# Attention and Snake feed-forward on one core: h tiles multiplied in pairs ahead of their Sin, matmuls grouped by tile shape, loads a chunk ahead, first chunks squared on ScalarE

## The chip, the cores and the metric

The kernel runs on one core of a Trainium2 chip. The time is that of the device, in microseconds (us); most executions of one kernel agree within one to two per cent. Each kernel was run several times, and one of the runs left a profile. The core has a matmul engine (TensorE, "PE" in the profile, with "PEld" for its weight loads), VectorE (DVE), ScalarE (ACT), GpSimd (POOL) and SyncE, which here only issues DMAs (SPq). Matmul results go to PSUM, here a ring of four pairs of banks.

## The reference

Eight batches, twelve heads, 448 tokens, head size 64. First attention with normalized q and k, then a feed-forward on the 3584 tokens, with the "snake" function between two matrix products.

```python
def rmsnorm(x, g):
    return x / np.sqrt(np.mean(x * x, axis=-1, keepdims=True) + 1e-06) * g
q_n, k_n = rmsnorm(q, g_q), rmsnorm(k, g_k)
scores = 1.0 / np.sqrt(64) * np.matmul(q_n, k_n.transpose(0, 1, 3, 2))
attn = np.exp(scores - max)            # row by row
attn = attn / (sum(attn) + 1e-09)
x = np.matmul(attn, v)                 # then to (3584 tokens, 768)

h = x @ w_in                           # 768 x 2048: the first product
s = np.sin(alpha * h)
g = h + s * s / (alpha + 1e-09)
out = g @ w_out                        # 2048 x 768: the second product
```

All inputs and the output are float32; the kernel multiplies in bf16.

## The kernel before

Per batch there is an *attention stretch* of six head pairs and then a *first product* with its snake. The second product of a batch is cut into steps of two matmuls ("fillers") that are put between the attention matmuls of the next batch. The normalization of the next batch's q and k ("norm tasks", three chunks of four heads per batch) runs in the background of the attention stretch. These are the parts that the change and the argument touch; cuts are marked with "...".

```python
    def norm_tasks(ci):                      # one chunk: 4 heads of q and of k
        def square(w):    ... nc.gpsimd.tensor_mul(st[w], qk[ci][:, w], qk[ci][:, w])
        def fold_g():         nc.gpsimd.tensor_mul(qk[ci][:, 1], qk[ci][:, 1], gg.to_broadcast([P, 2 * NJ, D]))
        def reduce(w):        nc.vector.reduce_sum(st["ms"][:, w, :], st[w], axis=AX.X)
        def rsqrt():      ... # Ln and Exp on ScalarE
        def scale(w):     ... nc.vector.tensor_mul(st["n"][...], qk[ci][:, w, js], st["inv"][...].to_broadcast(...))   # twice
        def transpose():  ... nc.sync.dma_start_transpose(out=qkT[pi]..., in_=st["n"]...)                             # twice
        return [lambda: square(0), lambda: square(1), lambda: (reduce(0), fold_g()), lambda: reduce(1), rsqrt,
                lambda: scale(0), lambda: scale(1), transpose]
...
    def attend(pi):
        av = bank_pair("av")
        for bank in range(2):                # bank 0: exp x v, bank 1: exp x ones (the row sums)
            for t in range(NT + 1):
                for hi in range(2):
                    ...                      # t < NT: tiles of 128 x 64, t == NT: tiles of 64 x 64
                    nc.tensor.matmul(av[r, bank, :S], lhsT, rhs, start=(t == 0), stop=(t == NT))
...
    def first_product(b):
        EARLY = 4                            # these are multiplied before the last head pair's xT is there, all but their last k tile
        ...
        for m in range(MT):                  # 16 h tiles of 128 x 448; two share a PSUM bank pair
            if m < EARLY:
                mm(tiles[m // 2], m, [KT - 1])
            else:
                if m % 2 == 0:
                    tiles[m // 2] = bank_pair("hps")
                mm(tiles[m // 2], m, range(KT))                        # 6 matmuls
            late.append(snake(b, tiles[m // 2][:, m % 2, :S], m))      # Sin on ScalarE, square, then VectorE
            if len(late) > 1:
                late.popleft()()
...
        for p in range(NP):                  # six head pairs
            scores(pi, 0); fill(part[1]); scores(pi, 1); bg(per_slot); fill(part[2] - part[1])
            if p:
                attend(pi - 1)
            fill(part[3] - part[2]); bg(per_slot); scores(pi, 2)
            fill(part[4] - part[3]); bg(per_slot); scores(pi, 3)
            fill(part[5] - part[4]); bg(per_slot)
            ...                              # batch 0: loads of w_in in four steps, then v and w_out
        bg(len(background)); fill(len(fillers))
        attend(b * NP + NP - 1)
        first_product(b)
```

## Time and profile before

The kernel took 692.86 us in the median of three runs. From the start times of the matmuls the span of the profiled run divides as follows (a stretch ends where the first matmul of the next one starts):

| stretch | before | after |
|---|---|---|
| until the first scores | 39.5 | 34.6 |
| attention of batch 0 | 72.4 | 44.2 |
| eight first products | 240.4 | 146.0 |
| attention of batches 1 to 6 | 275.6 | 256.7 |
| attention of batch 7 (nothing left to normalize) | 38.3 | 35.7 |
| last second product and store | 26.4 | 26.4 |
| span | 692.6 | 543.7 |

The page of the profile, its head. The digits are tenths of busy time in 40 slices of the span; PEclk is the clock granted to TensorE, and a half-clock window is a stretch in which the clock record grants half of full speed. In the profile's lines the tiles have the program's names: qkn and qkT are the normalized q and k before and after the transpose, sc the scores, expT their exponentials, av the product with v, xT the attention's result, hps the PSUM tiles of the first product, s and g_sb those of the snake, ops the accumulator of the second product.

```profile
span 692.6 us, 7553 instructions
...
PE 518.8 (75%) x2816; PEld 209.2 (30%) x2816; DVE 249.8 (36%) x352; ACT 342.1 (49%) x544; POOL 266.7 (39%) x253
...
PE   0043436789978995888878987888878986899786
...
PEclk9999656998999998999999995998999997999899
```

A PE that is 75% busy looks nearly full, but the figure is an average over stretches with different limits, and a matmul counts as busy longer than it keeps its successor waiting (352 ns of modelled duration against 189 ns from start to start).

The timeline of one period of a first product: start, duration, engine, line, operation, what it writes and reads, number of instructions, and in brackets the idle time before it and its releaser.

```profile
198.15 2.43 PE L261 MATMUL hps<-xT,w_in_sb 128*128 128x448 bf16 x12 [0.78 <-ACT s L242]
...
199.54 0.63 ACT L242 ACTIVATE s<-hps,alpha_sb 128x448 f32<-128x448 f32 x1 [1.44 <-PE hps L261]
...
200.69 0.62 ACT L242 ACTIVATE s<-hps,alpha_sb 128x448 f32<-128x448 f32 x1
201.35 2.43 PE L261 MATMUL hps<-xT,w_in_sb 128*128 128x448 bf16 x12 [0.78 <-ACT s L242]
```

The period is 201.35 - 198.15 = 3.20 us for 12 matmuls that need 12 x 0.189 = 2.27. PE multiplies the odd half of a pair and the even half of the next one, and then cannot start that pair's odd half until the Sin at 200.69 has read the even half: the two engines take turns. The waits view (engine and line, what it waited for, total us, times, longest) sums it up.

```profile
PE hps L261 <- ACT s L242: 56.1, 64, 1.7
...
PE sc L206 <- DMA qkT<-qkn: 51.7, 3, 39.5
...
PE hps L261 <- DVE xT L236: 10.5, 3, 3.9
```

In the attention the tightest stretch is batch 7. One head pair there, PE's timeline; the column after the names is the part of the array that a matmul uses, rows x columns, so "128*64" is half an array and two such matmuls run side by side (in this trace they start 4 ns apart).

```profile
611.54 1.06 PE L230 MATMUL av<-expT,vb 128*64 128x448 bf16 x8
612.54 1.06 PE L230 MATMUL av<-expT,ones 128*64 128x448 bf16 x8
613.54 0.50 PE L298 MATMUL ops<-w_out_sb,g_sb 128*128 128x384 bf16 x2
613.97 0.36 PE L206 MATMUL sc<-qkT 64*128 64x448 bf16 x2
614.26 0.82 PE L298 MATMUL ops<-w_out_sb,g_sb 128*128 128x384 bf16 x4
615.02 0.38 PE L208 MATMUL sc<-qkT 64*64 64x448 bf16 x2
615.33 0.82 PE L298 MATMUL ops<-w_out_sb,g_sb 128*128 128x384 bf16 x4
```

No line has an idle time in brackets, so PE bounds this stretch; from attend to attend it takes 6.31 us. Yet two second-product matmuls take 613.97 - 613.54 = 0.43 us before the shape changes, where 2 x 0.163 = 0.33 would do, and a pair of scores takes 0.29 us instead of 0.19. Each change of the tile shape costs about 0.1 us, and a head pair has 13 of them (an attend alone starts four of them: its 64x64 part comes once per bank).

### The profile page before, as it was taken

Reading aid. Unit: us, or ns where it says so; the run is one execution under the profiler, and the core shown is the slowest. Engines: PE = TensorE matmul, PEld = TensorE weight load, DVE = VectorE, ACT = ScalarE, POOL = GpSimd, SP = SyncE. Lnnn points to the kernel's source line nnn. Section 1 sums busy time; section 2 is a strip of 40 time slices with the busy share of each in tenths; the row PEclk is TensorE's granted clock in tenths of the full one; section 3 lists DMA queues with packets and bytes.
Section 4 is the critical chain, followed back from the end, with each engine's and each line's share of the span. In section 5 each row is a group of like instructions: output and inputs, shape, how many; then the busy total and the mean of one; then the engine's idle time right before and its main releaser. Section 6 shows DMA issues by size and latency. Waiting matters only on the chain.

```text
span 692.6 us, 7553 instructions
## 1 busy us (share of the span) xinstructions
PE 518.8 (75%) x2816; PEld 209.2 (30%) x2816; DVE 249.8 (36%) x352; ACT 342.1 (49%) x544; POOL 266.7 (39%) x253
## 2 busy tenths in 40 slices
PE   0043436789978995888878987888878986899786
PEld 0011102333333332333333332332333332333244
DVE  0543233344443425333543433333533333221331
ACT  0042226565656555565556644664556544765530
POOL 4842447283328303453436332543437332100210
PEclk9999656998999998999999995998999997999899
DMA  9259769865526544165407344355407342001002
GB/s 190 18 69 150 126 125 142 162 40 126 116 66 41 126 104 102 13 74 136 126 2 77 89 109 96 24 68 140 117 1 73 94 111 43 1 24 45 1 23 70
DMA packets 114406, 56.41 MB, mean 81 GB/s; under 512 B 93377, under 2 KB 110785, under 8 KB 114369
## 3 DMA queue, kind: packets, MB, share of 16 engines
q1 hardware_dynamic: 64432, 44.13, 27.6%
q0 software_dynamic: 49936, 11.80, 18.8%
q8 instruction: 22, 0.36, 0.2%
q14 instruction: 16, 0.12, 0.1%
HBM read 45.69 MB, written 11.01 MB: 82 GB/s over the span
## 4 chain that ended last, share of the span: by engine, by line
PE 45%; ACT 16%; POOL 14%; DMA 9%; DVE 7%; issue 5%; SPq 3%; DVEq 0%; ACTq 0%; POOLq 0%
PE hps L261 16%; PE ops L298 16%; ACT s L242 10%; PE av L230 9%; POOL sq L159 6%; DMA qk<-in_q_dram 6%; POOL vb L105 4%; ACT s L247 4%; PE sc L206 3%; POOL vb L109 3%; DVE qkn L177 3%; SPq L185 3%; DMA vb<-in_v_dram 2%; DVE ms L165 2%; PE sc L208 1%
## 5 line engine op out<-in xcount | busy, mean ns | idle before, releaser
L261 PE MATMUL hps<-xT,w_in_sb 128*128 128x448 bf16 x768 | 174.5, 378 | 66.6 <-ACT s L242 56.1
L298 PE MATMUL ops<-w_out_sb,g_sb 128*128 128x384 bf16 x896 | 186.7, 336 | 1.6 <-ACT expT L210 1.6
L159 POOL TENSOR_TENSOR sq<-qk 128x896 f32<-128x896 f32 x48 | 81.5, 1733 | 185.7 <-DMA qk<-in_q_dram 176.3
L210 ACT ACTIVATE expT<-sc 128x896 bf16<-128x896 f32 x144 | 126.6, 916 | 38.5 <-PE sc L206 37.5
L245 POOL TENSOR_TENSOR s<-s 128x448 f32<-128x448 f32 x64 | 59.7, 932 | 197.5 <-ACT s L242 182.1
L250 DVE SCALAR_TENSOR_TENSOR g_sb<-s,inv_alpha_sb,hps 128x448 bf16<-128x448 f32 x128 | 81.4, 677 | 140.8 <-ACT s L242 135.9
L242 ACT ACTIVATE s<-hps,alpha_sb 128x448 f32<-128x448 f32 x128 | 80.4, 628 | 103.3 <-PE hps L261 103.3
L261 PEld LDWEIGHTS <-w_in_sb 128*128 128x128 bf16 x768 | 78.1, 103 | 161.2 <-issue 105.9
L206 PE MATMUL sc<-qkT 64*128 64x448 bf16 x288 | 55.2, 385 | 66.0 <-DMA qkT<-qkn 51.7
L298 PEld LDWEIGHTS <-g_sb 128*128 128x128 bf16 x896 | 72.4, 99 | 77.4 <-issue 46.6
L165 DVE TENSOR_REDUCE ms<-sq 128x14 f32<-128x896 f32 x48 | 51.6, 1082 | 116.7 <-POOL sq L159 116.6
L236 DVE TENSOR_TENSOR xT<-av,rec 128x448 bf16<-128x448 f32 x48 | 29.8, 621 | 130.9 <-ACT rec L233 130.9
L177 DVE TENSOR_TENSOR qkn<-qk,inv 128x448 bf16<-128x448 f32 x96 | 64.3, 727 | 6.1 <-ACT inv L170 5.8
L230 PE MATMUL av<-expT,vb 128*64 128x448 bf16 (+1 forms) x384 | 57.7, 399 | 5.8 <-ACT expT L212 4.7
L232 ACT ACTIVATE rec<-av 128x448 f32<-128x448 f32 x48 | 26.1, 543 | 72.6 <-PE av L230 72.4
L169 ACT ACTIVATE inv<-ms,eps 128x28 f32<-128x28 f32 x24 | 7.6, 318 | 104.1 <-DVE ms L165 104.1
L230 PE MATMUL av<-expT,ones 128*64 128x448 bf16 (+1 forms) x384 | 56.9, 398 | 0.0
L162 POOL TENSOR_TENSOR qk<-qk,gg 128x896 f32<-128x896 f32 x24 | 50.4, 2100 | 1.9
L206 PEld LDWEIGHTS <-qkT 64*128 64x128 bf16 x288 | 15.0, 94 | 112.4 <-issue 59.6
L208 PE MATMUL sc<-qkT 64*64 64x448 bf16 x96 | 19.3, 395 | 28.5 <-ACT expT L210 22.1
L247 ACT ACTIVATE s<-s 128x448 f32<-128x448 f32 x64 | 36.9, 576 | 2.0
L105 POOL DMA_DIRECT2D vb<-in_v_dram x48 | 36.4, 788 | 0.8 <-POOLq L378 0.8
(21 smaller groups left out, 191.2 us busy)
## 6 DMA issues: line engine op xcount, KB each, us to landing
qk<-in_q_dram SPq DMA_DIRECT2D x24, 448.0 KB, 4.3
qk<-in_k_dram SPq DMA_DIRECT2D x24, 448.0 KB, 4.5
out_dram<-osb SPq DMA_DIRECT2D x56, 192.0 KB, 2.7
vb<-in_v_dram POOLq DMA_DIRECT2D x48, 96.0 KB, 3.8
w_in_sb<-in_moe_w_in_dram POOLq DMA_DIRECT2D x16, 192.0 KB, 5.5
w_out_sb<-in_moe_w_out_dram POOLq DMA_DIRECT2D x1, 3072.0 KB, 19.6
vb<-in_v_dram POOLq DMA_DIRECT2D x48, 16.0 KB, 2.7
qkT<-qkn SPq DMA_TRANSPOSE x48, 3.9
```

Of the source, the lines that this page charges most:

```text
L105: nc.gpsimd.dma_start(out=vb[b][jj * 64:jj * 64 + 64, t * H:(t + 1) * H, :], in_=tok[2 * t + jj])
L159: nc.gpsimd.tensor_mul(st[w], qk[ci][:, w], qk[ci][:, w])
L165: nc.vector.reduce_sum(st["ms"][:, w, :], st[w], axis=AX.X)
L177: nc.vector.tensor_mul(st["n"][:, w, :, hi, :], qk[ci][:, w, js], st["inv"][:, w, js].unsqueeze(2).to_broadcast([P, NJ, D]))
L206: nc.tensor.matmul(sc[:, hi, :S], kt[r, t * P:(t + 1) * P], qt[r, :], start=True, stop=True)
L210: nc.scalar.activation(expT[pi][:, 2 * t:2 * t + 2, :], sc[:, :, :S], ACT.Exp, scale=SCALE)
L230: nc.tensor.matmul(av[r, bank, :S], lhsT, rhs, start=(t == 0), stop=(t == NT))
L242: nc.scalar.activation(s1, hps, ACT.Sin, scale=alpha_sb[:, m, :])
L247: nc.scalar.activation(s2, s1, ACT.Square)
L250: nc.vector.scalar_tensor_tensor(g_sb[:, m, (b % 2) * S:(b % 2 + 1) * S], s2, inv_alpha_sb[:, m, :], hps, op0=ALU.mult, op1=ALU.add)
L261: nc.tensor.matmul(ps[:, m % 2, :S], w_in_sb[:, kt, m * P:(m + 1) * P], x[:, kt, :], start=(kt == 0), stop=(kt == KT - 1))
L298: nc.tensor.matmul(st["ps"][:, half, :HALF], lhsT, w_out_sb[:, m, half * HALF:(half + 1) * HALF], start=(m == 0), stop=(m == MT - 1))
```

## The change

The intent: let PE run through the first product without waiting for Sin; put matmuls of one tile shape together; start the work on q and k earlier; load with fewer, larger DMAs.

```diff
-    def load_qk(ci):
+    def load_qk(ci, eng=nc.sync):          # a chunk now takes its heads hi-major, v and w_in alike: longer runs per DMA
 ...
-    load_qk(1)
-    load_qk(2)
+    load_qk(1, nc.scalar)
+    load_qk(2, nc.scalar)
 ... # load_v: 4 DMAs per batch instead of 12; load_w_in: 2 DMAs in all instead of 16
-    def norm_tasks(ci):
+    def norm_tasks(ci, first=False):
 ...
-            nc.gpsimd.tensor_mul(st[w], qk[ci][:, w], qk[ci][:, w])
+            if first:
+                nc.scalar.activation(st[w], qk[ci][:, w], ACT.Square)
+            else:
+                nc.gpsimd.tensor_mul(st[w], qk[ci][:, w], qk[ci][:, w])
 ... # fold_g of the first chunks on VectorE; scale(1) in three instructions, for the new order of k's tokens
-        return [lambda: square(0), lambda: square(1), lambda: (reduce(0), fold_g()), lambda: reduce(1), rsqrt,
-                lambda: scale(0), lambda: scale(1), transpose]
+        if first:
+            return [lambda: square(1), lambda: (square(0), fold_g()), lambda: (reduce(1), reduce(0)), rsqrt,
+                    lambda: scale(0), lambda: scale(1), transpose]
+        return [lambda: (square(0), square(1)), fold_g, lambda: None, lambda: reduce(0), lambda: reduce(1), lambda: None,
+                rsqrt, lambda: (scale(0), scale(1), transpose())]
 ...
-        for bank in range(2):
-            for t in range(NT + 1):
+        for t in range(NT + 1):
+            for bank in range(2):
 ...
-        EARLY = 4
+        EARLY = 2
 ...
-        for m in range(MT):
-            if m < EARLY:
-                mm(tiles[m // 2], m, [KT - 1])
-            else:
-                if m % 2 == 0:
-                    tiles[m // 2] = bank_pair("hps")
-                mm(tiles[m // 2], m, range(KT))
-            late.append(snake(b, tiles[m // 2][:, m % 2, :S], m))
+        for i in range(MT // 2):
+            if i >= EARLY:
+                tiles[i] = bank_pair("hps")
+            for m in (2 * i, 2 * i + 1):
+                mm(tiles[i], m, [KT - 1] if i < EARLY else range(KT))
+            for m in (2 * i, 2 * i + 1):
+                late.append(snake(b, tiles[i][:, m % 2, :S], m))
 ...
+    gate = const.tile([P, 1], F32)
+    nc.gpsimd.tensor_copy(gate, qk[0][:, 0, 0, 0:1])      # GpSimd's loads wait for the first q
     load_v(0)
-    background.extend(norm_tasks(0))
-    bg(len(background))
     load_alpha()
-    for ci in range(1, NC):
-        background.extend(norm_tasks(ci))
+    load_w_in()
+    for ci in range(2):
+        for task in norm_tasks(ci, first=True):
+            task()
+    background.extend(norm_tasks(2, first=True))
 ...
-                background.append(lambda ci=ci: load_qk(ci))
-                background.extend(norm_tasks(ci))
+                tasks = norm_tasks(ci)
+                if ci + 1 < NC * B:
+                    tasks[0] = lambda t=tasks[0], ci=ci: (t(), load_qk(ci + 1))
+                background.extend(tasks)
 ...
-            scores(pi, 0); fill; scores(pi, 1); bg; fill; attend(pi - 1); fill; bg; scores(pi, 2); fill; bg; scores(pi, 3); fill; bg
+            scores(pi, 0); scores(pi, 1); attend(pi - 1); scores(pi, 3); bg; fill; bg; scores(pi, 2); fill; bg; fill; bg
```

(The last two lines stand for the loop body, one call per line in the kernel.)

## The prediction

> **What bounds the kernel now.** The program alternates eight attention stretches (each carrying the second product of the batch before) with eight first products. From the start times of the matmuls: first scores at 39.5 us; batch 0's attention to 111.9; attention of batches 1 to 7 together 314 us (44.0, 46.8, 44.7, 46.8, 46.6, 46.7, 38.3); the first products together 240 us (26.7 to 36.3); a last second product and store, 26 us.
>
> - *First product.* Timeline: 12 matmuls per h tile pair every 3.21 us, though matmuls follow each other at 0.189 us, so 12 need 2.27. The waits view: hps matmuls wait for the Sin 64 times, 56.1 us. A pair's odd half is written only after the even half's Sin has read the tile. ScalarE's own work is 1.8 us per pair.
> - *Attention.* Batch 7 shows the PE bound: 6.31 us per head pair without idle in the timeline. Of it 12 tiled pairs x 0.187 + 16 second-product matmuls x 0.163 = 4.84; the rest is 13 changes of tile shape, each about 0.1 us longer than a step without one (0.26 to 0.31 against 0.16 to 0.19). The Trainium skill (TensorEngine Tiling (Array Packing), Key Properties) says that a mode change drains the engine; the trace agrees. Batches 1 to 6 add 4 to 6 us: v loads hold POOL 8 us, then the squares, so reduce, rsqrt and the Exps behind it come late.
> - *Start.* POOL issues v loads until 20.3, then squares; scores start at 39.5. Batch 0 is a chain of qk loads, transposes, squares, reductions (PE busy 30.9 of 72.4 us, clock 0.77).
>
> **What the change does.**
> 1. First product: PE-bound at 2.27 us per pair, 96 matmuls = 18.1; I expect 18.7 per batch, 150 in all: -90 us, all on the chain.
> 2. Shape changes per head pair from 13 to 6: 4.84 + 6 x 0.105 = 5.5 us (6.4 with 128 fillers). v loads: 4 issues instead of 12; norm work spaced, loads a chunk ahead. With 3 us at each start for the last Sins and the table load: 38, 43 and 35.5 us per batch, 278 together: -35.
> 3. Start: qk0 lands at 8 to 9 us, Square on ACT, gg at 10 to 12 (was 11.7), then DVE fold 1.3, reductions 2.2, rsqrt 0.6, scales 3, transposes 6.7 as now: first scores near 26: -13.
> 4. Batch 0: ScalarE-bound at 4.5 to 5.5 us per pair plus late chunks while weights load: 42: -30.
>
> Added: six Squares and four DMA issues on ScalarE, three folds and some smaller scales on VectorE; each about 1 us.
>
> 26 + 42 + 150 + 278 + 26 = 522; plus 10 for cold-clock windows and collisions: **532 us, range 502 to 572**. Faster by over 2%: 0.97; within 2%: 0.02; slower by over 2%: 0.01.
>
> **What would show each step.** (1) the wait of hps for Sin drops from 56 us to a few; first products of 18 to 20 us. (2) about 5.5 and 6.4 us between attend groups; v issues on POOL near 3 us per batch. (3) first scores at 23 to 31 us. (4) batch 0's attention 35 to 50 us. Clock mean up from 0.919, since half-clock windows stand mostly where PE idles.
>
> **What would make it wrong.** The PSUM ring: four bank pairs, one held by the second product; if an h pair waits for VectorE's finish, or sc3 for an Exp, PE idles again. The large w_in load at the start could slow the qk loads and transposes on shared DMA engines. Alternating PSUM banks could cost something. ScalarE at 1.8 us per pair leaves little slack below 2.27. A first product could fall to half clock (0.374 us per matmul).

## The result

The changed kernel took 544.71 us in the median of four runs (537.96 to 547.16), the kernel before 694.5 us in four (690.98 to 698.18). The ratio is 0.781, with a 95% interval of 0.772 to 0.790. Executions over 1.5% slower than the fastest of the same kernel are left out of the means.

The head of the page after:

```profile
span 543.7 us, 7414 instructions
...
PE 458.2 (84%) x2816; PEld 214.7 (39%) x2816; DVE 293.5 (54%) x379; ACT 346.0 (64%) x550; POOL 206.2 (38%) x167
...
PE   0035589797989999897989999897989999899996
...
PEclk9996589799999999898998999898999999999998
```

PE is busier and its clock is fuller: half-clock windows in the clock record add up to 59 us, against 115 before. But VectorE is busy for 44 us more than before, with only 27 more instructions. That was not expected (the prediction reckoned with about 1 us for each of a few added instructions), and it comes back below.

A first product after, timeline:

```profile
149.81 6.41 PE L269 MATMUL hps<-xT,w_in_sb 128*128 128x448 bf16 x33
...
151.52 1.16 ACT L250 ACTIVATE s<-hps,alpha_sb 128x448 f32<-128x448 f32 x2 [0.45 <-PE hps L269]
...
153.79 1.16 ACT L250 ACTIVATE s<-hps,alpha_sb 128x448 f32<-128x448 f32 x2 [0.50 <-PE hps L269]
```

Now ScalarE is the one that waits, 0.5 us per pair, the period is 153.79 - 151.52 = 2.27 us, and PE runs without a gap. Every first product takes 18.2 to 18.3 us. What PE still waits for, by the waits view of after (the waits of hps for anything have gone):

```profile
PE sc L215 <- DMA qkT<-qkn: 34.6, 1, 34.6
...
PE ops L305 <- DVE g_sb L258: 11.4, 6, 1.9
PE sc L215 <- DVE xT L244: 10.9, 6, 2.8
```

In batch 7 a head pair now takes 5.53 us from attend to attend, and the fillers stand in two groups of eight (PE's timeline):

```profile
475.70 0.38 PE L238 MATMUL av<-expT,vb 128*64 128x448 bf16 x2
...
477.64 1.48 PE L305 MATMUL ops<-w_out_sb,g_sb 128*128 128x384 bf16 x8
...
479.35 1.47 PE L305 MATMUL ops<-w_out_sb,g_sb 128*128 128x384 bf16 x8
...
481.24 0.38 PE L238 MATMUL av<-expT,vb 128*64 128x448 bf16 x2
```

Two misses against the prediction: the start (34.6 us against about 26) and the attention of batches 1 to 7 (292.4 us against 278). The miss in the attention lies almost wholly in batches 1, 3 and 5 (42.1 to 42.8 us against 38); batches 2, 4 and 6, with a third more fillers, took 42.3 to 43.9 against 43, and batch 7 35.7 against 35.5. The rest came as foretold. The total is inside the predicted range.

The start, before and then after (timelines):

```profile
32.77 3.47 SPq L185 DMA_TRANSPOSE qkT<-qkn  x2
...
39.50 1.30 PE L206 MATMUL sc<-qkT 64*128 64x448 bf16 x6 [39.50 <-DMA qkT<-qkn]
```

```profile
16.54 0.25 DVE L132 RECIPROCAL inv_alpha_sb<-alpha_sb 128x16 f32<-128x16 f32 x1 [5.22 <-DMA alpha_sb<-in_moe_alpha_dram]
...
22.70 12.82 SPq L191 DMA_TRANSPOSE qkT<-qkn  x4
...
34.65 0.93 PE L215 MATMUL sc<-qkT 64*128 64x448 bf16 x4 [34.65 <-DMA qkT<-qkn]
```

VectorE stood for 5.2 us before a reciprocal whose data, 8 KB of alpha, had not landed, and the transposes then took 11.9 us from the first issue to the first scores instead of 6.7.

And the place where the attention loses (timeline of batch 1 after, the lines of VectorE and GpSimd and the PE instruction that waits):

```profile
125.14 1.15 DVE L178 TENSOR_TENSOR qkn<-qk,inv 128x448 bf16<-128x448 f32 x2
...
125.88 3.90 POOL L157 TENSOR_TENSOR sq<-qk 128x896 f32<-128x896 f32 x2 [9.28 <-DMA qk<-in_q_dram]
...
126.21 3.99 DVE L180 TENSOR_TENSOR qkn<-qk,inv 128x384 bf16<-128x384 f32 x2
...
129.86 2.27 POOL L161 TENSOR_TENSOR qk<-qk,gg 128x896 f32<-128x896 f32 x1
...
130.12 2.15 DVE L185 TENSOR_TENSOR qkn<-qk,inv 128x128 bf16<-128x128 f32 x1
...
132.20 0.61 DVE L244 TENSOR_TENSOR xT<-av,rec 128x448 bf16<-128x448 f32 x1
...
132.86 0.36 PE L215 MATMUL sc<-qkT 64*128 64x448 bf16 x2 [2.81 <-DVE xT L244]
```

The two scales of 128x448 take about 0.6 us each, though GpSimd's square begins while the second runs: the scale had come first. The next three begin when a product of GpSimd is under way: the two of 128x384 take 3.99 us together, and even the small one of 128x128 takes 2.15 us, where its mean free of GpSimd is 0.28. The xT product behind them is late, and it frees the PSUM bank that PE waits for: 2.81 us. The Trainium skill says this in *SBUF — State Buffer*, "Who interferes with whom" and "Summary: rules for kernel authors": a VectorE instruction with two SBUF inputs contends with a GpSimd instruction that reads SBUF, and the one that comes second is held until the first has finished. Over all scales of 128x448 in this trace, those that hardly overlap a GpSimd product take 0.62 us in the mean and those that mostly do 1.69 us (five that overlap one but began before it took 0.62); for the scales of 128x384 it is 0.55 and 2.21. Reductions, with one SBUF input, take 1.07 and 1.08 us. The trace agrees with the page. Whether this is what the attention stretch is short of is a matter for an experiment.

### The profile page after: what moved, and what is told of

The parts are those of the page before. It is cut to its first block, busy times and chain, and to the rows that moved or that the text cites. A ratio compares the mean times of both kernels' runs of the same rounds, so it can differ in the third digit from the quotient of the medians.

```text
span 543.7 us, 7414 instructions
## 1 busy us (share of the span) xinstructions
PE 458.2 (84%) x2816; PEld 214.7 (39%) x2816; DVE 293.5 (54%) x379; ACT 346.0 (64%) x550; POOL 206.2 (38%) x167
## 3 DMA queue, kind: packets, MB, share of 16 engines
q0 software_dynamic: 21808, 11.80, 17.5%
## 4 chain that ended last, share of the span: by engine, by line
PE 63%; DMA 14%; DVE 12%; issue 4%; ACT 3%; POOL 3%; SPq 1%; POOLq 0%; DVEq 0%
PE ops L305 23%; PE hps L269 22%; PE av L238 12%; DMA w_out_sb<-in_moe_w_out_dram 6%; PE sc L215 4%; DVE qkn L180 4%; DMA alpha_sb<-in_moe_alpha_dram 2%; DMA qk<-in_q_dram 2%; DMA qkT<-qkn 2%; DVE qkn L178 2%; DVE g_sb L258 2%; POOL s L253 2%; DVE ms L164 1%; DVE xT L244 1%; PE sc L217 1%
## 5 line engine op out<-in xcount | busy, mean ns | idle before, releaser
L305 PE MATMUL ops<-w_out_sb,g_sb 128*128 128x384 bf16 x896 | 168.9, 339 | 14.3 <-DVE g_sb L258 11.4
L269 PE MATMUL hps<-xT,w_in_sb 128*128 128x448 bf16 x768 | 146.7, 353 | 0.0
L305 PEld LDWEIGHTS <-g_sb 128*128 128x128 bf16 x896 | 83.6, 100 | 89.8 <-issue 41.7
L157 POOL TENSOR_TENSOR sq<-qk 128x896 f32<-128x896 f32 x42 | 74.3, 1791 | 105.9 <-DMA qk<-in_q_dram 64.6
L215 PE MATMUL sc<-qkT 64*128 64x448 bf16 x288 | 49.2, 382 | 53.4 <-DMA qkT<-qkn 34.6
L238 PE MATMUL av<-expT,vb 128*64 128x448 bf16 (+1 forms) x384 | 75.3, 386 | 9.8 <-ACT expT L219 4.1
L238 PE MATMUL av<-expT,ones 128*64 128x448 bf16 (+1 forms) x384 | 73.9, 378 | 0.0
L164 DVE TENSOR_REDUCE ms<-sq 128x14 f32<-128x896 f32 x48 | 51.2, 1076 | 22.5 <-POOL sq L157 22.5
L178 DVE TENSOR_TENSOR qkn<-qk,inv 128x448 bf16<-128x448 f32 x48 | 55.9, 1205 | 6.3 <-ACT inv L169 6.3
L215 PEld LDWEIGHTS <-qkT 64*128 64x128 bf16 x288 | 11.9, 95 | 91.2 <-issue 55.8
L180 DVE TENSOR_TENSOR qkn<-qk,inv 128x384 bf16<-128x384 f32 x48 | 46.1, 999 | 0.0
L309 DVE COPY osb<-ops 128x768 f32<-128x768 f32 x28 | 26.7, 954 | 34.1 <-PE ops L305 34.1
L238 PEld LDWEIGHTS <-vb 128*64 128x64 bf16 (+1 forms) x384 | 23.4, 111 | 53.4 <-issue 46.6
## 6 DMA issues: line engine op xcount, KB each, us to landing
w_out_sb<-in_moe_w_out_dram POOLq DMA_DIRECT2D x1, 3072.0 KB, 33.7
```

The costliest lines, as they stand in the source:

```text
L178: nc.vector.tensor_mul(n[:, :, hi, :], x[:, hi], inv[:, hi].unsqueeze(2).to_broadcast([P, NJ, D]))
L180: nc.vector.tensor_mul(n[:, :2 * NT, hi, :].rearrange("p (t jj) d -> p jj t d", jj=2), x[:, hi, :2 * NT].rearrange("p (jj t) d -> p jj t d ...
L215: nc.tensor.matmul(sc[:, hi, :S], kt[r, t * P:(t + 1) * P], qt[r, :], start=True, stop=True)
L269: nc.tensor.matmul(ps[:, m % 2, :S], w_in_sb[:, kt, m * P:(m + 1) * P], x[:, kt, :], start=(kt == 0), stop=(kt == KT - 1))
L305: nc.tensor.matmul(st["ps"][:, half, :HALF], lhsT, w_out_sb[:, m, half * HALF:(half + 1) * HALF], start=(m == 0), stop=(m == MT - 1))
```

## The experiments

Twelve kernels were run, each beside the kernel before on the same chip. All gave a correct result. Each time with its ratio:

| run | median us | ratio to before, 95% interval | first scores | batch 0 | products | batches 1-6 | batch 7 |
|---|---|---|---|---|---|---|---|
| the change | 544.71 | 0.781 (0.772-0.790) | 34.6 | 44.2 | 146.0 | 256.7 | 35.7 |
| e1_before_pairs | 627.83 | 0.911 (0.906-0.915) | 39.8 | 70.9 | 159.9 | 287.4 | 38.8 |
| e2_after_nopairs | 596.9 | 0.865 (0.861-0.870) | 34.0 | 44.4 | 213.1 | 240.1 | 34.8 |
| e3_after_nogroup | 550.99 | 0.801 (0.796-0.805) | 33.7 | 46.6 | 146.0 | 256.9 | 38.8 |
| e4_after_gate | 524.95 | 0.760 (0.755-0.766) | 33.8 | 43.0 | 146.0 | 237.2 | 37.3 |
| e5_after_recip | 543.51 | 0.789 (0.784-0.794) | 33.3 | 44.3 | 146.0 | 254.7 | 35.7 |
| e6_after_win_late | 545.19 | 0.791 (0.787-0.796) | 26.8 | 55.6 | 146.0 | 254.2 | 37.1 |
| e7_after_recip_win | 540.62 | 0.784 (0.778-0.789) | 21.1 | 55.3 | 146.0 | 253.8 | 37.3 |
| e8_gate_nogroup | 538.36 | 0.781 (0.777-0.785) | 33.6 | 44.2 | 146.0 | 247.7 | 38.9 |
| e9_gate_first | 509.66 | 0.736 (0.731-0.741) | 34.2 | 41.5 | 146.0 | 224.5 | 35.1 |
| e10_recip_cols | 539.36 | 0.779 (0.774-0.783) | 28.2 | 47.8 | 146.0 | 251.4 | 37.1 |
| e11_after_noahead | 566.28 | 0.817 (0.812-0.822) | 33.4 | 64.4 | 151.7 | 253.3 | 35.7 |
| e12_all | 500.05 | 0.725 (0.721-0.728) | 27.9 | 42.2 | 146.0 | 220.0 | 34.2 |

The stretches are those of the profiled run of each, in us, made as the table of before was. The calls were made at different times and not all on one chip, so small differences between rows of different calls (e1 to e4, e5 to e8, e9 to e11, e12, and the change itself) are not to be leaned on; the stretches are steadier than the totals.

### The pairs alone, and all but the pairs

In e1 the first product of the changed kernel is put into the kernel before; in e2 the first product of before into the changed kernel.

```diff
-        EARLY = 4
-        for m in range(MT): ... mm(one h tile) ... snake
+        EARLY = 2
+        for i in range(MT // 2): ... mm(both h tiles of the pair) ... snake, snake
```

(e1 as shown, on the kernel before; e2 the other way round, on the changed kernel.)

> The kernel before with the new first product alone (both halves of an h tile multiplied, then their two Sins). Theory (the Sin wait held PE, and with it went PE's half-clock windows inside the products): each first product falls to 18.3 us as in the changed kernel, all eight from 240 to 146 us, so about 600 us in all. Rival (only the wait itself goes, half-clock windows stay): 60 us of waits go, 632 us, with products of 20 to 26 us. Rival 2 (the time is given back in the attention stretches, because ScalarE and PSUM are then late): attention of batches 1 to 7 grows from 314 by 10 us or more.

> The changed kernel with the first product of before. Theory: plus 85 to 100 us, to about 635 us, the waits of hps matmuls for Sin back at 56 us and half-clock windows back inside the products (products of 27 us and more). Rival: plus 60 us only, because with the new load order the clock stays up.

The line of the groups view for the matmuls of the first product (count, busy us, mean ns, then the idle time before them and what ended it), in e1:

```profile
L261 PE MATMUL hps<-xT,w_in_sb 128*128 128x448 bf16 x768 | 150.7, 358 | 9.8 <-DVE xT L236 9.8
```

and in e2:

```profile
L269 PE MATMUL hps<-xT,w_in_sb 128*128 128x448 bf16 x768 | 156.9, 352 | 56.9 <-ACT s L250 56.9
```

The Sin wait goes with the pairs and comes back without them, so that part of the theory stands. The sizes were off in both runs. The first theory's totals (600 and 635 us) fell; the measured 628 and 597 us lie near those of the rivals (632 and 605), but not for the rivals' reason alone. In e1 the products fall by 80.5 us, and 12 us of it come back in the attention of batches 1 to 7 (314 to 326 us), as the second rival said. In e2 products of 26.7 us each make 213 us, not 240: the other parts of the change alone take 27 us out of them. They have no half-clock window in a product (here the theory was wrong) and no wait for xT; the kernel before has both. So of the 94 us in the products, 67 need the pairs once the rest is there, and 27 come with the better background work.

e2 shows where the pairs give back. Its attention of batches 1 to 7 takes 275 us, the changed kernel's 292. The time from the first matmul of such a stretch to its first attend is 5.9 to 6.5 us in e2 and 6.7 to 10.6 us in the changed kernel; over the seven batches it is 42.8 against 59.2 us, which is 16 of the 17 us. With the pairs PE leaves the product earlier than ScalarE and VectorE do, and what it saved it partly waits out at the start of the next stretch. (One of the seven, batch 1, also waits 3 us for w_out and then runs at half clock: its first attend comes after 10.6 us in this trace and after 6.7 in those of e5 to e7, which have the same attention, so that only some 12 of the 16 us are sure to come of the early end.)

### The grouping by tile shape

In e3 the order of before returns, in the attend and in the loop over head pairs.

```diff
-        for t in range(NT + 1):
-            for bank in range(2):
+        for bank in range(2):
+            for t in range(NT + 1):
...
-            scores 0, 1, attend, scores 3; bg; fill; bg; scores 2; fill; bg; fill; bg
+            scores 0; fill; scores 1; bg; fill; attend; fill; bg; scores 2; fill; bg; scores 3; fill; bg
```

> The changed kernel with the matmul order of before in the attention (fillers in five places, attend bank by bank): 13 changes of tile shape per head pair instead of 6. Theory (a change costs 0.1 us on a PE-bound stretch): batch 7 goes back from 5.54 to 6.3 us per head pair, and in all 48 pairs less batch 0's six the loss is 42 x 0.75 = 32 us: 576 us. Rival (in batches 1 to 6 VectorE's late scales set the pace, so that the order costs little there): plus 10 to 18 us, most of it in batch 7.

Batch 7 goes from 35.7 to 38.8 us, its head pairs from 5.53 to 6.31 us: the cost of 0.1 us per change of shape is right. But batches 1 to 6 stay at 257 us. The grouping is worth next to nothing there as the changed kernel stands (e5 to e7, with the grouping, have 253.8 to 254.7 us), and the loss is only some 5 to 13 us (span and ratio). The rival's picture is right; of its 10 to 18 us only the lower part is within what was measured.

### Keeping GpSimd's products away from VectorE's scales

In e4 a tiny copy on GpSimd ahead of each chunk's squares reads the last element that the scales of the chunk before wrote. It changes no result; it makes GpSimd wait.

```diff
             else:
+                if w == 0:
+                    nc.gpsimd.tensor_copy(gate, last_n["n"][:, 1, NJ - 1, 0, 0:1])
                 nc.gpsimd.tensor_mul(st[w], qk[ci][:, w], qk[ci][:, w])
 ... # scale() keeps its output tile in last_n["n"]
```

> The changed kernel with one 128x1 copy on GpSimd ahead of each chunk's squares that reads the last scale of the chunk before: squares and the g product can no longer run beside VectorE's scales. Theory (a scale, which has two SBUF inputs, is held while GpSimd reads SBUF: 0.62 us alone, 1.7 to 2.2 us beside GpSimd in the changed kernel, and that is why batches 1 to 6 still lose some 4 to 6 us each): scales of 128x448 fall to a mean under 0.75 us, VectorE's busy time by 40 us, attention of batches 1 to 6 by 15 to 30 us in all: 515 to 530 us. Rival (the stall in these batches is the late landing of the qk load, or ScalarE): time within 1 per cent of the changed kernel, or longer as squares come later.

It took 524.95 us, 20 us less than the changed kernel in the medians (some 14 by the two ratios), in the expected range; batches 1 to 6 lose 19.5 us of attention, from 256.7 to 237.2 (17.5 us against e5, where w_out is in time for batch 1 as it is here). The groups view of the changed kernel and of e4 for the scales:

```profile
L178 DVE TENSOR_TENSOR qkn<-qk,inv 128x448 bf16<-128x448 f32 x48 | 55.9, 1205 | 6.3 <-ACT inv L169 6.3
...
L180 DVE TENSOR_TENSOR qkn<-qk,inv 128x384 bf16<-128x384 f32 x48 | 46.1, 999 | 0.0
```

```profile
L181 DVE TENSOR_TENSOR qkn<-qk,inv 128x448 bf16<-128x448 f32 x48 | 29.2, 649 | 6.3 <-ACT inv L171 6.3
...
L183 DVE TENSOR_TENSOR qkn<-qk,inv 128x384 bf16<-128x384 f32 x48 | 24.5, 550 | 2.2 <-POOL qk L163 2.2
```

VectorE's busy time falls from 293.5 to 245.7 us, and the order on GpSimd is now what the copy asks for (its timeline in batch 1 of e4; the scales of this chunk ended at 110.1):

```profile
110.17 0.19 POOL L158 CAST gate<-qkn 128x1 f32<-128x1 bf16 x1 [4.89 <-DVE qkn L188]
110.31 3.32 POOL L159 TENSOR_TENSOR sq<-qk 128x896 f32<-128x896 f32 x2
```

An instruction added, and VectorE's busy time and the stretches fall together: the changed kernel's attention was short of VectorE, held by GpSimd. PE's wait for xT at the scores (10.9 us above) is gone from e4's waits. The first four periods from one attend to the next are 5.53 us in batches 1, 3 and 5, where the changed kernel had one of 8.5 us among them. In batches 2, 4 and 6, where more fillers make a period 6.51 us long, one of 7.5 to 8.0 us goes: the scales are held for about 7 us in every one of batches 1 to 6, but the longer periods hide most of it. The rival (the late load, or ScalarE) falls.

e8 then repeats the undoing of the grouping, on top of the gate.

```diff
 the edit of e3, on the kernel of e4
```

> The gate on GpSimd's squares (with it the changed kernel took 525 us) and the matmul order of before in the attention (with the changed kernel it cost 7 us). Theory (grouping by tile shape is worth 0.75 us per head pair where PE sets the pace, and was hidden in batches 1 to 6 because VectorE's held scales set it): without the grouping the gated kernel loses 25 to 35 us, attention of batches 1 to 7 back from 274 to 300 or more. Rival (the order is worth little in itself; other waits always fill in): it loses 5 to 12 us, as the changed kernel did.

It took 538.36 us, 13 us more than e4 (ratio 0.781 against 0.760). So the grouping is worth more once VectorE keeps up, as the theory says, but only half of what it foretold; the rival's upper end is nearly right. The trace tells why. The first four of the five periods from attend to attend in a batch do get shorter, by 0.78 us in batches 1, 3, 5 and 7 (6.31 to 5.53). The fifth gets 0.5 us longer there (4.54 to 5.05). And the grouped order starts each batch later: from the stretch's first matmul to its first attend it takes 58.3 us over seven batches in e4 and 50.4 in e8. The theory had counted all six head pairs.

### The start of a batch

Why does the grouped order start late? PE's timeline at the start of batch 2 in e4, with one line of ScalarE:

```profile
148.99 0.55 PE L219 MATMUL sc<-qkT 64*128 64x448 bf16 x4
...
149.89 0.38 PE L221 MATMUL sc<-qkT 64*64 64x448 bf16 x2 [0.35 <-DVE g_sb L262]
...
150.88 1.28 ACT L340 ACT_TABLE_LOAD   x1
...
152.15 3.32 PE L309 MATMUL ops<-w_out_sb,g_sb 128*128 128x384 bf16 x10 [1.89 <-DVE g_sb L262]
```

Three scores take two free bank pairs and the first one that the product gives back. The fillers' accumulator needs the fourth, which VectorE still reads for the last h tiles. PE waits 1.89 us, and then ten matmuls take 3.32 us where 10 x 0.163 is 1.63: the clock record has a window at half clock from 151.9 for 3.4 us. (Six of the seven batches have such a window; batch 1 has the same wait of 1.89 us without one, and its first eight fillers take 1.46 us.) In e9 the first head pair of each batch puts fillers right after its first scores.

```diff
             scores(pi, 0)
+            if p == 0:
+                fill(part[2]); scores(pi, 1); fill(part[3] - part[2]); scores(pi, 3); bg; bg; scores(pi, 2)
+            else:
                 scores(pi, 1); attend(pi - 1); scores(pi, 3); bg; fill(part[2]); bg; scores(pi, 2); fill(part[3] - part[2])
             bg; fill(part[4] - part[3]); bg
```

> The gated kernel (525 us; its attention stretches are 37.3 and 42.3 us) with another order in the first head pair of each batch alone: a share of the fillers right after the first scores, the rest of the pair's scores after them. In the gated kernel PE stands idle 1.9 us there, since three scores have taken the free PSUM bank pairs and the fillers' accumulator waits for VectorE to finish the last h pair (fillers start 3.2 us after the first product's end), and then the clock is halved for 3.4 us. Theory (that PSUM wait is what the grouped order gives back of its gain): fillers start 0.5 us after the product's end, half-clock windows in these places go, 2 to 3 us per batch in batches 1 to 7: 505 to 512 us. Rival (ScalarE's last Sins and its table load set the start of the batch whatever PE does): within 5 us of the gated kernel.

The timeline at the start of batch 1 in e9:

```profile
93.95 0.36 PE L219 MATMUL sc<-qkT 64*128 64x448 bf16 x2
...
94.25 1.47 PE L309 MATMUL ops<-w_out_sb,g_sb 128*128 128x384 bf16 x8
```

Fillers begin 0.3 us after the first scores and run at full clock. It took 509.66 us, 15 us less than e4 in the medians; attention of batches 1 to 7 went from 274.5 to 259.6 us, and no half-clock window is left between batch 0's end and the last matmul. ScalarE's table load still comes 1.9 us after the first scores, as in e4, so the rival falls. This was the other thing that the changed kernel's attention was short of.

### The start of the program

Three kernels tell alpha's part from that of w_in.

```diff
 e5 and e7:
     def load_alpha():
         nc.sync.dma_start(out=alpha_sb, in_=...)
-        nc.vector.reciprocal(inv_alpha_sb, alpha_sb)
 ...
             if b == 0 and p == 2:
+                nc.vector.reciprocal(inv_alpha_sb, alpha_sb)
                 load_v(1)
 e6 and e7:
-    load_w_in()
     for ci in range(2):
         for task in norm_tasks(ci, first=True):
             task()
+    nc.gpsimd.tensor_copy(gate, qkT[3][:, 0, 0:1])
+    load_w_in()
```

> The changed kernel with the reciprocal of alpha taken out of VectorE's way at the start (the load of alpha stays where it is; the reciprocal is issued in batch 0's third head pair). In the changed kernel VectorE sat from 11.3 to 16.5 us before it. Theory A (the transposes of the first chunk take about 12 us from issue however early they are issued): first scores 5 us earlier, near 29 us. Theory B (the transposes' 256-byte packets take turns with the 4096-byte packets of w_in, and come through only when w_in has drained near 32 us): first scores at 32 to 34 us, time within 3 us of the changed kernel.

> The changed kernel with the loads of w_in issued only when the transposes of chunks 0 and 1 have landed. Theory B: alpha lands sooner (about 10 us instead of 16.5), the transposes take some 7 us instead of 12: first scores at 23 to 27 us instead of 34.6; the w_in packets then fall in batch 0, whose attention may grow from 44 us by 0 to 6: in all 3 to 10 us less than the changed kernel. Theory A: first scores near 29 us from alpha alone, transposes still near 12 us.

> Both of the two before this one. Theory B: hardly more than the late w_in alone gives, as alpha then lands before it is in the way: first scores at 22 to 26 us, in all 3 to 10 us less than the changed kernel. Theory A: as the sum of both.

In e5 the first transpose is issued at 17.3 us instead of 22.7, as it should be, and the first scores start at 33.3: the transposes now take 16 us. Theory B holds there, and theory A falls. In e6 each transpose lands 3.5 to 3.8 us after its issue, and the first scores start at 26.8 us. But alpha landed no sooner in e6 (14.0 us after its issue, 13.6 in the changed kernel), so it was not w_in that delayed alpha, and that part of theory B was wrong. The DMA records of the changed kernel agree: w_in's first packet comes at 15.3 us, when alpha's last is passing. They also show what alpha met. Its 2048 packets of 4 bytes stand on SyncE's queue behind q, k and g: only about 50 packets of 4 bytes pass there before 9 us, 1709 from 9 to 12 us, and the last 366 need until 15.4 us, while 1200 packets of v pass from 12 to 15 us. In the kernel before, where alpha was issued at 36.3 us, it landed 6.4 us later. No run moved v or alpha, so that v and the queue delayed it is read from the records and not tested. Hence e7 is not "hardly more" than e6 but 5.7 us better at the start: 21.1 us. The two delays add up once w_in is out of the way, and hide one another when it is not.

None of this shows in the total. In e6 and e7 batch 0's attention grows from 44 to 55 us, more than the 0 to 6 us that were expected, since the transposes of the third chunk now meet w_in (up to 18 or 19 us to landing): the wait has moved. The ratios, 0.784 to 0.791, cannot be told from the changed kernel's 0.781 (0.772 to 0.790).

How the transposes lose can be counted in the DMA records of the trace, by packet size, in windows of 4 us:

| kernel, window | 256-byte packets (transposes) | packets of w_in, size | mean ns of one, 256-byte and w_in |
|---|---|---|---|
| e5, 20 to 24 us | 148 | 197, 4096 bytes | 30, 323 |
| e5, 24 to 28 us | 195 | 192, 4096 bytes | 31, 322 |
| e5, 32 to 36 us (w_in has landed) | 2647 | 1, 4096 bytes | 26, 322 |
| e10, 24 to 28 us | 606 | 614, 1024 bytes | 30, 96 |
| e10, 28 to 32 us | 634 | 606, 1024 bytes | 30, 96 |

The Trainium skill, *DMA: Bandwidth & Descriptors*, "Queues, rings and completion order", says that an engine goes round the queues that have work, a packet at a time. The trace agrees to the point that the two kinds of packets come nearly one for one, 195 to 192 (a packet of that page holds several descriptors; whether a record of the trace is such a packet is not shown). The size of the packet then sets the shares of time, and a stream of 256-byte packets beside one of 4096 gets about a tenth. e10 tests that by cutting w_in's packets, at the same place, on the kernel of e5.

```diff
-        for hi in range(2):
-            nc.gpsimd.dma_start(out=w_in_sb[hi * 64:hi * 64 + 64], in_=rows[hi])
+        for c in range(0, D_FF, 512):
+            for hi in range(2):
+                nc.gpsimd.dma_start(out=w_in_sb[hi * 64:hi * 64 + 64, :, c:c + 512], in_=rows[hi, :, :, c:c + 512])
```

> The kernel with the late reciprocal (first scores at 33.3 us, transposes 10 to 16 us from issue to landing) and w_in loaded at the same place in eight loads of 512 columns instead of two of 2048, so that its packets have 1024 bytes instead of 4096. Theory (packets of the queues take turns, so the transposes' share of the DMA engines grows as the other packets shrink): the first transposes land in 5 to 9 us, first scores at 23 to 28 us, in all up to 8 us less. Rival (transposes wait until w_in has drained, whatever the size of its packets): first scores at 31 us or later.

With packets of a quarter the size three times as many transpose packets pass in 4 us, and the first scores start at 28.2 us, 5 us earlier than in e5 and just above the 23 to 28 us expected. The rival, which wanted 31 us or later, falls. The fastest transpose took 8.9 us, the upper end of what was expected, and batch 0 grew by 3.5 us, so in all the gain is small: 539.36 us, a ratio of 0.779 against 0.789.

### The load a chunk ahead

e11 issues each load of q and k at the start of its own chunk again.

```diff
-                if ci + 1 < NC * B:
-                    tasks[0] = lambda t=tasks[0], ci=ci: (t(), load_qk(ci + 1))
+                tasks[0] = lambda t=tasks[0], ci=ci: (load_qk(ci), t())
```

> The changed kernel with each qk load issued at the start of its own chunk again, not a chunk ahead. Theory (the load ahead lets GpSimd square the next chunk while VectorE scales this one; the late load kept them apart): scales of 128x448 under 0.85 us in the mean instead of 1.2, VectorE's busy time down by 25 us or more; but reductions then wait for the late squares, so the time may go either way: 525 to 550 us. Rival (what brings them together is the order of the tasks, not the load): scales stay at 1.2 us.

The groups view of e11 for the first scales (1205 ns in the changed kernel):

```profile
L178 DVE TENSOR_TENSOR qkn<-qk,inv 128x448 bf16<-128x448 f32 x48 | 31.1, 688 | 5.8 <-ACT inv L169 5.8
```

The scales of 128x448 fall to 0.69 us in the mean and VectorE's busy time to 247.5 us: it is the load ahead that brings squares and scales together, and the rival falls. But the total is 566 us, above the range that was expected. Batch 0 alone takes 64.4 us (44.2 with the load ahead), and the first products 5.7 us more; by the waits view of the whole span the reductions wait 125 us for squares (22.5 with the load ahead) and rsqrt 86 us for reductions (28.5). Batches 1 to 6 are only 3 us better than in the changed kernel, as one wait has been exchanged for another. The load ahead is worth keeping; the collision that it causes is what the gate takes away, at no loss.

### All that helped

e12 has the gate, the early fillers (with four filler steps more in the first head pair), the late reciprocal and w_in in eight loads.

```diff
 the edits of e4, e5, e9 and e10, and in the loop over head pairs:
+            if n_fill:
+                x0 = n_fill // NP + 4
+                rest = n_fill - x0
+                quota = x0 if p == 0 else (rest * p) // (NP - 1) - (rest * (p - 1)) // (NP - 1)
```

> All that helped, together: the gate, the fillers early in a batch's first head pair (with four of the 48 or 64 filler steps moved there from the later pairs), the late reciprocal and w_in in eight loads. Theory (each removes another wait): 500 to 508 us, against 510 with the gate and the early fillers; first scores near 28 us, attention of batches 1 to 7 at 250 to 258 us instead of 260. Rival (the start's gain is eaten by batch 0 as in the runs with the late w_in): 507 to 511 us.

It took 500.05 us in the median of six runs (498.48 to 501.92), at the lower end of what was expected, and beats both kernels: ratio 0.725 (0.721 to 0.728) to before. First scores at 27.9 us and batch 0 at 42.2 us, so here the start's gain is not eaten by batch 0.

## Why the prediction was right

The prediction was right: 544.71 us against 532, in the range of 502 to 572. Its sum of stretches was 522 plus 10 for half-clock windows and collisions. The profile's 543.7 us differs from 522 by 8.6 us at the start, 14.4 in the attention of batches 1 to 7, 2.2 in batch 0 and -4 in the products, which together make 21.2 of the 21.7 us (the rest is rounding and the last product). The 10 us set aside cover half of that; the rest is inside the range because the range was wide, not because these terms were known.

1. *First product: right.* 18.7 us per batch was foretold, 18.3 measured, and the wait for Sin went from 56 us to none. The reason was right too (e1, e2). What the prediction did not see is that 27 of the 94 us come from the rest of the change (e2). That PE's earlier end costs some 12 to 16 us at the starts of the next stretches it did allow for, with 3 us at each start for the last Sins and the table load. In e9 the table load stays where it was and the time comes back: what cost it was the wait for the PSUM bank pair that the last snake still holds, and the half clock after it. The size of this allowance was partly luck.
2. *Attention of batches 1 to 7: direction right, size too large by 14 us* (292.4 against 278; -21.5 us instead of -35). The period of 5.5 us per head pair was right to the digit (5.53; 6.51 with 128 filler matmuls against 6.4). The term that failed is "norm work spaced, loads a chunk ahead": it was counted as a pure gain. In the trace the load ahead lets GpSimd's products run beside VectorE's scales, which are then held (0.62 to 1.7 us and more), and one head pair per batch takes 7.5 to 8.5 us. With the gate alone batches 1, 3 and 5 take 35.7 to 37.3 us (38 foretold), batches 2, 4 and 6 42.3 to 42.4 (43), and the sum is 274.5, near the 278 that was foretold (e4). The skill's page states the rule; the prediction did not apply it.
3. *Start: direction right, size too large by 8.6 us* (first scores at 34.6 against 26). Failed step: "transposes 6.7 as now". With w_in's packets in the way they took 11.9 us, and alpha's reciprocal held VectorE for another 5.2 us that the prediction left out. With both out of the way (e7) the first scores come at 21.1 us, so the sum's other terms were some 5 us too long, and the two delays cost more than the miss shows. The prediction named w_in's load among what would make it wrong.
4. *Batch 0: right*, 44.2 against 42.
5. *What would make it wrong.* The PSUM ring was named rightly: "PE idles again" is the wait of 1.9 us at the start of each batch (e9). The alternation of banks could not be seen to cost anything (5.53 us against the 5.5 worked out without such a cost). No first product fell to half clock. v's issues take GpSimd 2.9 us per batch, as foretold (3), and the mean clock rose from 0.919 to 0.947.

## What to carry to other kernels

Where two engines share a tile by halves, fill both halves before the reader starts, so that the writer always has another tile to go on with; here that alone took 80 us out of 240. Work that is moved earlier meets other work: after such a change look for instructions whose mean duration has grown, as here VectorE's scales beside GpSimd's products, and for transfers that share the DMA engines with larger packets. When a stretch becomes shorter on one engine, look at the first microseconds of the next stretch, because the others have not finished: an order that is best in the middle of a loop need not be best in its first pass.

## What the Trainium skill lacked or had wrong

- *TensorEngine Tiling (Array Packing)*, "Key Properties", says that a change of mode drains the engine and gives no size. Here it adds about 0.1 us: 0.26 us from a second-product matmul to one of another shape instead of 0.163, and 0.28 us instead of 0.19 between tiled pairs; 13 against 6 changes make 6.31 against 5.53 us per head pair.
- *SBUF — State Buffer*, "Who interferes with whom", is right here (two SBUF inputs are held, one is not: 0.62 to 1.69 us for scales, 1.07 to 1.08 for reductions). It lacks that VectorE's mean durations in a profile show the hold as busy time, not as waiting: the gate alone took 48 us off VectorE's busy time (293.5 to 245.7), and the waits view of the changed kernel names GpSimd for none of the scales.
- *DMA: Bandwidth & Descriptors*, "Queues, rings and completion order", has the turn-taking by packets, but not what follows for a DMA transpose beside a bulk load: its packets of 256 bytes passed one for one with those of 4096 (195 to 192 in 4 us), and four transposes took up to 15.9 us to land that land in 3.5 to 3.8 us alone. Packets of 1024 bytes in the bulk load tripled the transposes' rate.
- *TensorE: Matmul & The Clock Gate*, "HAM oscillation — how this bites in real kernels", gives the rule that idle gaps should not exceed about 3.4 us. Here a window of 3.4 us at half clock followed a stretch in which no single idle gap was longer than 1.9 us (e4, at 151.9 us), and it went when the gap was filled (e9). For shorter gaps the page gives no length, and here a gap of 1.9 us was followed by such a window in six batches of seven.
- *DMA: Bandwidth & Descriptors*, "Rules for kernel authors", warns of loads with one element to a run but gives no time for one. Here alpha, 8 KB in 2048 packets of 4 bytes, took 11.8 to 14.2 us to land at the changed program's start, with w_in's load behind it or not, and 6.4 us in the kernel before, where it was issued later.
